# A double-to-single rounding of weight tiles: three VectorE operations in place of five, in a retention and two-layer FFN kernel

## The chip, the cores and the metric

One Trainium2 chip, one core of it. The metric is the device time of one execution of the whole program in microseconds (us). The kernel before took 897.66 us, the median of three runs (896.89 to 899.72).

Engines are named as the profile names them: PE is TensorE (PEld its weight loads), DVE VectorE, ACT ScalarE, POOL GpSimd, SP the engine that issues the DMAs.

## The reference

```python
scores = scale * np.matmul(q, k.transpose(0, 1, 3, 2))          # 4 x 8 heads, 576 positions, 64 wide
ret = scores * Dmat[None, :, :, :]                              # causal decay gamma ** (i - j)
x = np.matmul(ret, v)                                           # -> 2304 tokens x 512
h = x @ w_in;  g = P(h) / (Q(h) + 1e-06);  x = g @ w_out        # layer 1, P cubic, Q quadratic in |h|
h = x @ w_in2; r = np.maximum(h, 0.0)
out = (s * (r * r) + b) @ w_out2                                # layer 2
```

Both layers are 512 to 2048 to 512 wide. The weights arrive as float64, the output is float32.

## The kernel before, in words

**Retention.** Sixteen pairs of heads (`retention`), each with scores, a decay mask, a chunked state and the product with v. DVE makes `pm` (L211), `spre` (L223) and `x` (L242) of each pair; ACT rounds `x` to `xh` (L244) and POOL writes the rest `xl` (L245) and scales `vn` (L190). Nearly all of it stands in program order (`tc.keep_in_program_order`). The loads of pair p+4 are issued at pair p.

**The two layers.** `ffn` walks over units: a block of 256 or 512 tokens by one of 16 slices of 128 hidden columns in each layer, 80 units a layer. `emit_in` (L322 to L324) makes `h` in PSUM with 12 matmuls, from high and low parts of both operands; `rational_*` turn it into `g` in layer 1 (ACT, DVE and POOL), `relu2` in layer 2; `emit_out` (L407) multiplies by the slice's second matrix into `o`, and `evac` adds that to `acc` (L417 or L419). There are `H_BUFS = 4` tiles `h` in PSUM, and in layer 1 the reciprocal is written back into `h` (L356), so unit u+4 can begin on PE only when the last DVE operation of unit u (L363) has read it. Four more PSUM tiles hold `o`.

**The weights.** Tile kf (32 of them, 128 x 1024 doubles, 1 MB) holds both matrices of a slice. `w_load` brings it into one of three `raw` buffers; `w_cut` rounds it. A double is seen as two 32-bit words, `lo` and `hi`, each with a stride of two words. Before, the cut is: ACT takes the absolute value of `hi` read as a float into `wm` (L114), DVE rounds `lo` (L115), clamps `wm` (L117), shifts it (L119), puts the sign in (L121) and ors in the top bits of `lo` (L124, into `hi`). Then ACT copies the result to the fp32r tile `wh` (L130), POOL writes the rest `wl` (L131), and the next load goes out on SP. There is one `wm` buffer (`WTMP_BUFS = 1`), and a slot of `wh` and `wl` comes free when the last unit of tile kf-5 has been multiplied.

**The order.** `w_cut` is a generator that yields after each DVE step. In retention, `steps` chains the cuts of tiles 0 to 2, and each pair from 3 on takes one step (two from 14 on); between the last step of a tile and the first of the next there is no yield. In `ffn`, `emit_cuts` spreads `CUT_STEPS` steps of a tile evenly over the units up to its first use. These calls set only the order of writing there: a scheduler, which is given the program with modelled costs, then sets each engine's queue, and the engines run their queues in order.

Of the kernel before, what the change touches and what calls it, by code (L numbers as in the profile page):

```python
# [11 lines left out]
I32 = mybir.dt.int32  # L12
U32 = mybir.dt.uint32
I64 = mybir.dt.int64
AF = mybir.ActivationFunctionType
ALU = mybir.AluOpType
# [17 lines left out]
G_BUFS = 3  # L34
T_BUFS = {"ta": 2, "tq": 2, "tt": 4}
H_BUFS = 4
CUT_STEPS = 5
W_FIRST = 3
LAG_NS = (5000.0, 4000.0)

# [2 lines left out]
def retention_ffn_kernel(ctx, tc, a, b, s2, b2, w, qkv, maskv, gdec, out):  # L43
    nc = tc.nc
# [31 lines left out]
    def f32(t):  # L76
        return t.bitcast(F32)
# [10 lines left out]
    def next_load(eng=nc.sync, pin=free):  # L88
        if w_ahead:
            w_load(w_ahead.pop(0), eng, pin)  # L90
# [11 lines left out]
    def w_cut(kf, pinned=False):  # L102

        words = w_raw.pop(kf).bitcast(I32).rearrange("p (n two) -> p n two", two=2)
        lo, hi = words[:, :, 0].bitcast(U32), words[:, :, 1]
        f = hi.bitcast(F32)
        m = wtmp.tile([P, 2 * DM], F32, tag="wm", name=f"wm{kf}")
        t = m.bitcast(I32)  # L110

        rest = tc.keep_in_program_order if pinned else free
        pin = tc.keep_in_program_order if kf < W_FIRST + RAW_BUFS else free
        pin(nc.scalar.activation(m, f, AF.Abs))  # L114
        pin(nc.vector.tensor_scalar(lo, lo, 2.0 ** 28, 2.0 ** 32 - 256, op0=ALU.add, op1=ALU.min))  # L115
        yield
        pin(nc.vector.tensor_scalar(m, m, 2.0 ** -15, None, op0=ALU.max))  # L117
        yield
        rest(nc.vector.tensor_scalar(t, t, 5, 2, op0=ALU.logical_shift_left, op1=ALU.logical_shift_right))  # L119
        yield  # L120
        rest(nc.vector.scalar_tensor_tensor(out=t, in0=hi, scalar=-0x40000000, in1=t,  # L121
                                            op0=ALU.bitwise_and, op1=ALU.bitwise_or))
        yield
        rest(nc.vector.scalar_tensor_tensor(out=hi.bitcast(U32), in0=lo, scalar=29, in1=t.bitcast(U32),  # L124
                                            op0=ALU.logical_shift_right, op1=ALU.bitwise_or))
        wh, wl = w_slots[kf % W_BUFS]
        whf, wlf = (x.rearrange("p w c f -> p (w c f)") for x in (wh, wl))
        for which in range(2):
            w_t[kf, which] = (wh[:, which], wl[:, which])
        rest(nc.scalar.copy(whf, f))  # L130
        nc.gpsimd.tensor_tensor(out=wlf, in0=f, in1=f32(whf), op=ALU.subtract)  # L131
        next_load()
# [8 lines left out]
    def retention(actx):  # L141
# [113 lines left out]
        for p in range(1, IN_BUFS):  # L255
            loads(p)
            if p == 2:
                next_load(nc.sync, pin)

        steps = (s for kf in range(W_FIRST) for s in w_cut(kf, True))  # L260


# [29 lines left out]
    def ffn(fctx):  # L292
# [166 lines left out]
        def emit_cuts(u):  # L459

            while items and items[0][1] <= u:
                need, free, kf = items.pop(0)
                assert free < need
                cuts.append([need, CUT_STEPS, w_cut(kf)])
            todo, n = 0, 0
            for need, left, _ in cuts:
                todo += left
                n = max(n, -(-todo // max(need - 1 - u, 1)))
            for _ in range(n):
                cuts[0][1] -= 1  # L470
                next(cuts[0][2], None)
                if not cuts[0][1]:
                    cuts.pop(0)
# [107 lines left out]
```

## Time and profile before

| | |
|---|---|
| three runs | 896.89, 897.66, 899.72 us |
| span of the profiled execution, first to last instruction | 893.9 us |
| busy: PE, PEld | 865.7 (97%), 729.2 us |
| busy: DVE, ACT, POOL | 610.2, 529.4, 360.9 us |
| mean granted clock of PE | 0.997 |

The profile gives the profiled execution by its span; no device time of its own stands beside it. The median lies 3.8 us above that span, which is taken as what lies around it. Times in the views are counted from the span's start. Retention lasts until about 82 us, layer 1 until about 520, layer 2 until the end.

### The profile page before, as it was taken

The numbers are of one execution on the slowest core, as the hardware profiler recorded it, in microseconds if no ns is written. First come the engines' busy times: TensorE is split into PE (matmuls) and PEld (weight loads), VectorE is DVE, ScalarE is ACT, GpSimd is POOL, SyncE is SP. The second block draws the span as 40 slices with busy tenths as digits, with TensorE's granted clock in tenths as the row PEclk, the third lists the DMA queues.
The fourth block names the chain that finished last, engine by engine and source line by source line (L and its number), as shares of the span: only waits on it lengthen the run. The fifth ranks groups of instructions, "written<-read, shape, count | busy, mean of one in ns | idle before, by whom it ended". The sixth has DMA issues, their size and how long they took to land.

```text
span 893.9 us, 12550 instructions
## 1 busy us (share of the span) xinstructions
PE 865.7 (97%) x4896; PEld 729.2 (82%) x4896; DVE 610.2 (68%) x905; ACT 529.4 (59%) x876; POOL 360.9 (40%) x248
## 2 busy tenths in 40 slices
PE   6999999899999999999999899999999999999998
PEld 6988788678788878878888688888888888888886
DVE  4897997999988898888989861545544464333334
ACT  1234997877877877688887664544444444343332
POOL 3776764557565655565788800011111111100000
PEclk9999999999999999999999999999999999999999
DMA  9992110111111101111111110111111110000013
GB/s 339 376 350 96 48 48 1 48 47 48 48 47 48 48 0 48 48 48 48 48 48 48 48 48 0 48 48 48 48 48 47 48 35 14 1 0 1 8 64 141
DMA packets 15418, 58.52 MB, mean 65 GB/s; under 512 B 2176, under 2 KB 2688, under 8 KB 11264
## 3 DMA queue, kind: packets, MB, share of 16 engines
q1 hardware_dynamic: 15360, 57.74, 17.8%
q8 instruction: 38, 0.62, 0.3%
q14 instruction: 20, 0.16, 0.1%
HBM read 53.01 MB, written 4.72 MB: 65 GB/s over the span
## 4 chain that ended last, share of the span: by engine, by line
PE 56%; DVE 17%; ACT 3%; DMA 3%; POOL 2%; issue 1%; DVEq 0%; ACTq 0%
PE o L407 29%; PE h L322 9%; PE h L324 9%; PE h L323 9%; DMA raw<-in_w_dram 3%; DVE acc L419 2%; DVE wm L121 2%; POOL wl L131 2%; DVE raw L124 2%; DVE tt L361 1%; DVE tt L350 1%; DVE h L362 1%; DVE tt L363 1%; DVE wm L119 1%; DVE tt L351 1%; DVE wm L117 1%
## 5 line engine op out<-in xcount | busy, mean ns | idle before, releaser
L322 PE MATMUL h<-xl,wh 128*128 128x512 f32 (+1 forms) x640 | 236.9, 370 | 6.2 <-DVE tt L363 6.1
L324 PE MATMUL h<-xh,wh 128*128 128x512 f32 (+1 forms) x640 | 236.2, 369 | 0.0
L323 PE MATMUL h<-xh,wl 128*128 128x512 f32 (+1 forms) x640 | 236.2, 369 | 0.0
L131 POOL TENSOR_TENSOR wl<-raw,wh 128x1024 fp32r<-128x1024 f32 x32 | 80.4, 2512 | 282.1 <-ACT wh L130 258.2
L380 DVE TENSOR_SCALAR tt<-ta,s_sb,b_sb 128x512 f32<-128x512 f32 (+1 forms) x80 | 47.0, 587 | 153.4 <-ACT ta L379 153.3
L322 PEld LDWEIGHTS h<-xl,wh 128*128 128x128 f32 x640 | 121.0, 189 | 29.2 <-DVE tt L363 4.4
L344 POOL TENSOR_TENSOR tq<-tq,ta 128x512 f32<-128x512 f32 (+1 forms) x80 | 102.1, 1277 | 97.0 <-ACT tq L343 95.1
L323 PEld LDWEIGHTS h<-xh,wl 128*128 128x128 f32 x640 | 121.0, 189 | 20.6
L324 PEld LDWEIGHTS h<-xh,wh 128*128 128x128 f32 x640 | 120.9, 189 | 20.6
L407 PE MATMUL o<-gl,wh 128*128 128x512 f32 (+1 forms) x320 | 118.4, 371 | 4.7 <-POOL gl L373 3.2
L373 POOL TENSOR_TENSOR gl<-tt,gh 128x512 fp32r<-128x512 f32 (+1 forms) x80 | 108.5, 1357 | 35.6 <-ACT gh L368 30.6
L378 ACT ACTIVATE ta<-h 128x512 f32<-128x512 f32 (+1 forms) x80 | 44.5, 557 | 127.7 <-PE h L324 127.6
L407 PE MATMUL o<-gh,wl 128*128 128x512 f32 (+1 forms) x320 | 117.7, 368 | 0.0
L407 PE MATMUL o<-gh,wh 128*128 128x512 f32 (+1 forms) x320 | 116.6, 368 | 0.0
L407 PE MATMUL o<-wh,gl 128*128 128x512 f32 x288 | 112.3, 390 | 0.4 <-DVE gl L383 0.4
L407 PE MATMUL o<-wh,gh 128*128 128x512 f32 x288 | 112.1, 389 | 0.0
L407 PE MATMUL o<-wl,gh 128*128 128x512 f32 x288 | 94.0, 390 | 1.7 <-DVE acc L419 1.7
L383 DVE TENSOR_TENSOR gl<-tt,gh 128x512 fp32r<-128x512 f32 (+1 forms) x80 | 53.2, 665 | 41.1 <-ACT gh L382 41.1
L382 ACT CAST gh<-tt 128x512 fp32r<-128x512 f32 (+1 forms) x80 | 46.3, 579 | 54.3 <-DVE tt L380 52.3
L407 PEld LDWEIGHTS o<-gl,wh 128*128 128x128 f32 x320 | 60.2, 188 | 17.7 <-POOL gl L373 4.7
L419 DVE TENSOR_TENSOR acc<-acc,o 128x512 f32<-128x512 f32 (+1 forms) x114 | 69.6, 650 | 3.3 <-PE o L407 3.3
L361 DVE SCALAR_TENSOR_TENSOR tt<-tt,aneg,h 128x512 f32<-128x512 f32 (+1 forms) x80 | 54.9, 687 | 20.6 <-ACT h L356 20.6
(51 smaller groups left out, 1414.9 us busy)
## 6 DMA issues: line engine op xcount, KB each, us to landing
raw<-in_w_dram SPq DMA_DIRECT2D x32, 1024.0 KB, 4.8
xT<-in_qkv_dram SPq DMA_DIRECT2D x16, 576.0 KB, 8.2
vn<-in_qkv_dram SPq DMA_DIRECT2D x16, 320.0 KB, 8.2
out_dram<-acc SPq DMA_DIRECT2D x18, 256.0 KB, 2.1
kn<-in_qkv_dram SPq DMA_DIRECT2D x16, 256.0 KB, 7.6
mv<-in_maskv_dram SPq DMA_DIRECT2D x1, 310.0 KB, 4.2
odec<-in_gdec_dram SPq DMA_DIRECT2D x1, 256.0 KB, 5.8
a_sb<-in_moe_a_dram SPq DMA_DIRECT2D x1, 2.0 KB, 9.5
```

The lines of the kernel that those rows point to most:

```text
L131: nc.gpsimd.tensor_tensor(out=wlf, in0=f, in1=f32(whf), op=ALU.subtract)
L322: nc.tensor.matmul(ps, lhsT=wh[:, c, :], rhs=xl[:, c, r], start=c == 0, stop=False)
L323: nc.tensor.matmul(ps, lhsT=wl[:, c, :], rhs=xh[:, c, r], start=False, stop=False)
L324: nc.tensor.matmul(ps, lhsT=wh[:, c, :], rhs=xh[:, c, r], start=False, stop=c == NC - 1)
L344: nc.gpsimd.tensor_tensor(out=tq, in0=tq, in1=ta, op=ALU.mult)
L361: nc.vector.scalar_tensor_tensor(out=tt, in0=tt, scalar=aneg[:, 0:1], in1=r, op0=ALU.add, op1=ALU.mult)
L373: nc.gpsimd.tensor_tensor(out=gl, in0=tt, in1=f32(gh), op=ALU.subtract)
L380: nc.vector.tensor_scalar(tt, ta, s2_sb, b2_sb, op0=ALU.mult, op1=ALU.add)
L382: nc.scalar.copy(gh, tt)
L383: nc.vector.tensor_tensor(out=gl, in0=tt, in1=f32(gh), op=ALU.subtract)
L407: nc.tensor.matmul(ps, lhsT=lh, rhs=rh, start=st and x == 0, stop=sp and x == 2)
L419: nc.vector.tensor_tensor(out=at, in0=at, in1=ps, op=ALU.add)
```

## The change

`w_cut` is written with three DVE steps. ACT multiplies `hi`, read as a float, by 2^-112 (`Copy` with a scale, where `Abs` stood); DVE turns `lo` into its top three bits by a multiplication and a minimum (L115), shifts `wm` left by three and ors those bits in (new L117, one operation with two tensor inputs), and puts the sign of `hi` in (new L120, also two inputs). L117 and L119 of before, both with one tensor input, have no counterpart. `CUT_STEPS` goes from 5 to 3, which changes where the steps are written between the units. Lines after the cut are lower by 4 in the new file.

```diff
-CUT_STEPS = 5
+CUT_STEPS = 3
...
-        t = m.bitcast(I32)
+        t = m.bitcast(U32)
...
-        pin(nc.scalar.activation(m, f, AF.Abs))
-        pin(nc.vector.tensor_scalar(lo, lo, 2.0 ** 28, 2.0 ** 32 - 256, op0=ALU.add, op1=ALU.min))
+        pin(nc.scalar.activation(m, f, AF.Copy, scale=2.0 ** -112))
+        pin(nc.vector.tensor_scalar(lo, lo, 2.0 ** -29, 7.0, op0=ALU.mult, op1=ALU.min))
         yield
-        pin(nc.vector.tensor_scalar(m, m, 2.0 ** -15, None, op0=ALU.max))
+        rest(nc.vector.scalar_tensor_tensor(out=t, in0=m.bitcast(U32), scalar=3, in1=lo,
+                                            op0=ALU.logical_shift_left, op1=ALU.bitwise_or))
         yield
-        rest(nc.vector.tensor_scalar(t, t, 5, 2, op0=ALU.logical_shift_left, op1=ALU.logical_shift_right))
-        yield
-        rest(nc.vector.scalar_tensor_tensor(out=t, in0=hi, scalar=-0x40000000, in1=t,
+        rest(nc.vector.scalar_tensor_tensor(out=hi.bitcast(U32), in0=hi.bitcast(U32), scalar=0x80000000, in1=t,
                                             op0=ALU.bitwise_and, op1=ALU.bitwise_or))
-        yield
-        rest(nc.vector.scalar_tensor_tensor(out=hi.bitcast(U32), in0=lo, scalar=29, in1=t.bitcast(U32),
-                                            op0=ALU.logical_shift_right, op1=ALU.bitwise_or))
```

The queues of all engines are laid out anew. PE has the same 4896 matmuls; their interleaving of `h` and `o` differs in layer 1. In retention the cuts of tiles 0 to 2 now end at pair 9, not 14, and on SP `raw2` stands right behind `raw1`, ahead of the inputs of pair 8 (before, behind those of pair 11), `raw4` ahead of those of pair 12 and `raw5` ahead of those of pair 14 (both before behind those of pair 15).

The first place is ACT at the head of layer 1, from the operation on tile 3 on (`ta0`, `tq0` belong to unit 0, `ta1`, `tt1` to unit 1). Before:

```order
L114 ACTIVATE wm3_1083<-raw3_602 128x1024
L342 ACTIVATE ta0_1099<-h0_1086 128x512
L345 ACTIVATE tt0_1101<-h0_1086,aneg_72 128x512
L343 ACTIVATE tq0_1100<-ta0_1099,babs_73 128x512
L342 ACTIVATE ta1_1131<-h1_1118 128x512
L345 ACTIVATE tt1_1133<-h1_1118,aneg_72 128x512
```

Now:

```order
L114 ACTIVATE wm3_1077<-raw3_585 128x1024
L338 ACTIVATE ta0_1093<-h0_1080 128x512
L341 ACTIVATE tt0_1095<-h0_1080,aneg_72 128x512
L339 ACTIVATE tq0_1094<-ta0_1093,babs_73 128x512
L126 CAST wh3_86<-raw3_585 128x1024
L338 ACTIVATE ta1_1125<-h1_1112 128x512
```

The copy `wh3` moved from behind unit 3's exponential to a place ahead of unit 1's first operation; on DVE all three steps of tile 3 now stand ahead of unit 0's first operation, where one of five stood, and the first step of tile 6 stands ahead of unit 1's last operation.

The second place is DVE in layer 1 at unit 15, which with tiles 6 and 7 shares the queue there; its last operation (L363, now L359) lets unit 19 begin on PE. Before:

```order
L351 SCALAR_TENSOR_TENSOR tt15_1781<-tt15_1781,aneg_72,h15_1766 128x512
L117 TENSOR_SCALAR wm6_1941<-wm6_1941 128x1024
L119 TENSOR_SCALAR wm6_1941<-wm6_1941 128x1024
L121 SCALAR_TENSOR_TENSOR wm6_1941<-raw6_1236,wm6_1941 128x1024
L350 TENSOR_TENSOR tt16_1825<-tt16_1825,h16_1810 128x512
L124 SCALAR_TENSOR_TENSOR raw6_1236<-raw6_1236,wm6_1941 128x1024
L361 SCALAR_TENSOR_TENSOR tt15_1781<-tt15_1781,aneg_72,h15_1766 128x512
L362 SCALAR_TENSOR_TENSOR h15_1766<-tq15_1780,h15_1766 128x512
L351 SCALAR_TENSOR_TENSOR tt16_1825<-tt16_1825,aneg_72,h16_1810 128x512
L350 TENSOR_TENSOR tt17_1873<-tt17_1873,h17_1858 128x512
L115 TENSOR_SCALAR raw8_1892<-raw8_1892 128x1024
L363 SCALAR_TENSOR_TENSOR tt15_1781<-h15_1766,tt15_1781 128x512
```

Now:

```order
L347 SCALAR_TENSOR_TENSOR tt15_1771<-tt15_1771,aneg_72,h15_1756 128x512
L117 SCALAR_TENSOR_TENSOR wm6_1929<-wm6_1929,raw6_1146 128x1024
L346 TENSOR_TENSOR tt16_1819<-tt16_1819,h16_1804 128x512
L120 SCALAR_TENSOR_TENSOR raw6_1146<-raw6_1146,wm6_1929 128x1024
L347 SCALAR_TENSOR_TENSOR tt16_1819<-tt16_1819,aneg_72,h16_1804 128x512
L357 SCALAR_TENSOR_TENSOR tt15_1771<-tt15_1771,aneg_72,h15_1756 128x512
L358 SCALAR_TENSOR_TENSOR h15_1756<-tq15_1770,h15_1756 128x512
L117 SCALAR_TENSOR_TENSOR wm7_2161<-wm7_2161,raw7_1284 128x1024
L359 SCALAR_TENSOR_TENSOR tt15_1771<-h15_1756,tt15_1771 128x512
L115 TENSOR_SCALAR raw8_1790<-raw8_1790 128x1024
L120 SCALAR_TENSOR_TENSOR raw7_1284<-raw7_1284,wm7_2161 128x1024
```

Between the two operations on unit 15 stand four operations on weights before (one of them on tile 8) and three now; both steps of tile 7 moved forward, around unit 15's last operation.

The third place is DVE where layer 1 ends: `o77` are the PSUM tiles that PE needs again there, `wm21` is tile 21. Before:

```order
L115 TENSOR_SCALAR raw21_4983<-raw21_4983 128x1024
L363 SCALAR_TENSOR_TENSOR tt79_4807<-h79_4792,tt79_4807 128x256
L117 TENSOR_SCALAR wm21_5393<-wm21_5393 128x1024
L380 TENSOR_SCALAR tt81_4929<-ta81_4928,s2_sb_74,b2_sb_75 128x256
L119 TENSOR_SCALAR wm21_5393<-wm21_5393 128x1024
L121 SCALAR_TENSOR_TENSOR wm21_5393<-raw21_4983,wm21_5393 128x1024
L419 TENSOR_TENSOR acc_1082<-acc_1082,o77_0_4824 128x512
```

Now:

```order
L115 TENSOR_SCALAR raw21_4791<-raw21_4791 128x1024
L117 SCALAR_TENSOR_TENSOR wm21_5317<-wm21_5317,raw21_4791 128x1024
L376 TENSOR_SCALAR tt82_4943<-ta82_4942,s2_sb_74,b2_sb_75 128x256
L415 TENSOR_TENSOR acc_1076<-acc_1076,o77_0_4793 128x512
```

Ahead of the first add of `o77` stand two operations on tile 21 where four stood.

## Rows read from the trace of the kernel before

**Rows 1.** Busy time by stage: length, then busy us (instructions) per engine, PE clock, DMA.
```profile
22.35:82.00 59.65, 56.37 (x963) 51.83 (x960) 50.97 (x70) 18.57 (x32) 44.45 (x28) 1.00 0.76 290
...
156.45:178.80 22.35, 18.39 (x80) 14.94 (x79) 21.54 (x25) 19.37 (x33) 12.26 (x8) 0.92 0.13 48
...
82.00:520.00 438.00, 425.01 (x2037) 354.72 (x2037) 389.83 (x573) 351.69 (x582) 282.66 (x201) 1.00 0.13 46
...
520.00:871.65 351.65, 351.65 (x1631) 294.36 (x1630) 149.21 (x231) 150.19 (x248) 26.71 (x11) 1.00 0.08 29
```

**Rows 2.** Who waited for whom, whole span: total us, times, longest us.
```profile
DVE raw L115 <- DMA raw<-in_w_dram: 22.6, 17, 3.1
...
PE h L322 <- DVE tt L363: 6.1, 4, 4.0
...
PE o L407 <- POOL gl L373: 3.2, 4, 1.2
PE o L407 <- DVE acc L419: 3.2, 3, 1.7
```

**Rows 3.** Groups by line, whole span: busy us, mean ns, then idle before.
```profile
L124 DVE SCALAR_TENSOR_TENSOR raw<-raw,wm 128x1024 uint32<-128x1024 uint32 x32 | 46.0, 1437 | 0.1
L121 DVE SCALAR_TENSOR_TENSOR wm<-raw,wm 128x1024 int32<-128x1024 int32 x32 | 45.2, 1412 | 0.4
...
L119 DVE TENSOR_SCALAR wm<-wm 128x1024 int32<-128x1024 int32 x32 | 30.9, 966 | 0.4
L117 DVE TENSOR_SCALAR wm<-wm 128x1024 f32<-128x1024 f32 x32 | 28.5, 891 | 5.7 <-ACT wm L114 5.6
L115 DVE TENSOR_SCALAR raw<-raw 128x1024 uint32<-128x1024 uint32 x32 | 28.4, 887 | 22.7 <-DMA raw<-in_w_dram 22.6
```

**Rows 4.** Timeline of PE in retention: start us, length us, what.
```profile
28.23 1.33 PE L208 MATMUL sc<-xT 64*128 64x128 f32 x20
...
36.20 1.33 PE L208 MATMUL sc<-xT 64*128 64x128 f32 x20
```

**Rows 5.** Timeline of DVE in retention: the x of five pairs.
```profile
28.63 0.75 DVE L242 TENSOR_TENSOR x<-pv,odec 128x576 f32<-128x576 f32 x1
...
37.25 0.75 DVE L242 TENSOR_TENSOR x<-pv,odec 128x576 f32<-128x576 f32 x1
...
41.72 0.74 DVE L242 TENSOR_TENSOR x<-pv,odec 128x576 f32<-128x576 f32 x1
...
47.15 0.74 DVE L242 TENSOR_TENSOR x<-pv,odec 128x576 f32<-128x576 f32 x1
...
81.99 0.76 DVE L242 TENSOR_TENSOR x<-pv,odec 128x576 f32<-128x576 f32 x1 [1.36 <-PE pv L239]
```

**Rows 6.** Timeline at the head of layer 1, three engines.
```profile
83.61 2.01 DVE L115 TENSOR_SCALAR raw<-raw 128x1024 uint32<-128x1024 uint32 x1
...
86.25 0.81 ACT L343 ACTIVATE tq<-ta,babs 128x512 f32<-128x512 f32 x1
...
92.31 0.69 DVE L363 SCALAR_TENSOR_TENSOR tt<-h,tt 128x512 f32<-128x512 f32 x1
...
97.26 0.50 PE L407 MATMUL o<-gl,wh 128*128 128x512 f32 x1 [1.19 <-POOL gl L373]
```

**Rows 7.** The loads of weight tiles until 120 us.
```profile
DMA to landing us min/median/max: 4.7/5.3/9.5
```

**Rows 8.** Timeline around unit 15, POOL, DVE and PE.
```profile
156.18 2.45 POOL L131 TENSOR_TENSOR wl<-raw,wh 128x1024 fp32r<-128x1024 f32 x1
...
157.19 1.99 DVE L117 TENSOR_SCALAR wm<-wm 128x1024 f32<-128x1024 f32 x1 [0.88 <-ACT wm L114]
...
167.72 0.47 PE L322 MATMUL h<-xl,wh 128*128 128x512 f32 x1 [3.96 <-DVE tt L363]
```

**Rows 9.** Timeline of DVE where layer 1 ends.
```profile
492.58 1.45 DVE L117 TENSOR_SCALAR wm<-wm 128x1024 f32<-128x1024 f32 x1
...
495.26 1.78 DVE L119 TENSOR_SCALAR wm<-wm 128x1024 int32<-128x1024 int32 x1
```

## The prediction

> **What bounds the kernel now.** I read the busy time by stage first, then who waited for whom, then the timelines at the places where PE waits.
>
> The stages [rows 1]: in layer 2 (520 to 871.65) PE is busy for all 351.65 us, so no cheaper cut can shorten it, though 9 of the 32 tiles are cut there. In retention from 22.35 to 82 PE is busy 56.37 of 59.65 us and DVE 50.97. In the stretch with layer 1 (82 to 520) PE is busy 425.0 of 438.0 us and DVE 389.8, or 89%. So PE is the bound, and what the change can give back is PE's idle time where DVE is dense: 13.0 us there, some us in retention, and a stretch at the lower clock: from 156.45 to 178.8 the mean granted clock is 0.92. Between the two levels of 2.4 and 1.2 GHz that is 22.35 x 0.08 x 2 = 3.6 us at the lower one, behind PE's only idle time of about 4 us in the layers, and 1.8 us of work lost.
>
> The waits [rows 2] say who ended PE's idle time: DVE's last operation of a unit (6.1 us in 4 waits, one of 4.0), POOL's `gl` (3.2 in 4), DVE's adds to `acc` (3.2 in 3). Together 12.5 of the 13.0 us.
>
> **The change part by part.**
>
> *What DVE loses.* The two operations that go cost 28.5 and 30.9 us in 32 tiles [rows 3], together 59.4 of DVE's 610.2 us. The three that stay are forms that the trace knows: L115 by its mean of 0.89 us, the two with two inputs by 1.41 and 1.44. A cut falls from 5.6 to 3.7 us. The new arithmetic of L115 and the scaled copy on ACT are in no row. For L115 the bounds are the 0.89 us of today (same form, type and stride) and 1.44 (the rate of two inputs); I take 0.89, since only the arithmetic differs; the upper bound would give 17.6 of the 59.4 us back. ACT's copy I take at the old cost, nothing, with POOL's port and table loads unchanged: the program has one table load, as before. Most of the 59.4 us lies beside PE work and buys nothing: 9 cuts lie in layer 2. It counts at the following places.
>
> *Retention: -1.5 us.* PE needs (36.20 - 28.23) / 2 = 3.99 us a pair where nothing holds it [rows 4]. From the `x` at 28.63 to that at 81.99 there are 12 periods in 53.4 us [rows 5]; at PE's pace 47.8. The 5.5 us over are periods with a long DVE step: 4.47 us for one with a single two-input step (37.25 to 41.72), 5.43 for one with two steps (41.72 to 47.15). Now four periods have one two-input step (+0.4 each) and two have two steps (+1.2, a little under the 1.44 of before), the other six none: 1.6 + 2.4 = 4.0 over, so 1.5 less. Against it, `raw2`, `raw4` and `raw5` go out ahead of inputs that followed or preceded them otherwise. DMA is 0.76 busy there already [rows 1]; the inputs of pairs 14 and 15 come up to two tiles later and POOL's scaling of pair 15 gets close to its need. Bounds: +2.0 (DMA sets the pace) and -4.0 (only the two double steps remain, and their second one is short).
>
> *Head of layer 1: +0.8 us.* ACT's copy `wh3` now stands behind `tq0` (86.25 to 87.06 [rows 6]) and waits for all three steps of tile 3 on DVE. The first of these ran from 83.61 to 85.6; two more at 1.2 end about 88.0, the copy about 89.2, so unit 1's operations on ACT start 1.5 us later than before, and unit 0's last on DVE ends about 95.4, not 93.0 (92.31 + 0.69). Unit 4 on PE starts behind that, now at 95.4 and not at 93.0. But behind unit 4 PE idled 1.19 us for `gl0` and went on at 97.26; `gl0` is now ready at 98.0, and PE comes at 98.1. So 0.8 is what stays. Next in line is the first step of tile 6, whose load `wl3` releases at about 91.7; with the shortest landing of 4.7 us [rows 7] it is there at 96.4, and DVE comes to it at 97.5. Bounds: 0 and +2.6.
>
> *Unit 15: -4.2 us.* This is the long wait. Unit 19 could start on PE at 163.8 and waits until 167.72 for unit 15's last operation [rows 8]. Before it stand the operations of tile 6. The first, at 157.19, took 1.99 us where its kind takes 0.69 alone: POOL's `wl` ran until 158.63. I let the new two-input step end at 158.63 + 1.2 = 159.8, and add the rest of the queue by the pitch of its neighbours: 0.6 + 1.15 + 0.7 + 0.65 + 0.65 + 1.15 (tile 7) + 0.6 = 165.3. PE's wait falls from 4.0 to 1.6 us. The mean clock from 82 to 520 rounds to 1.00, so it falls nowhere else for long, and the other waits in the layers' rows are 1.7 us and less [rows 1, 2]; so the 1.8 us at the lower clock go too: 2.4 + 1.8. Bounds: 0 and -5.8.
>
> The Trainium skill, page "SBUF — State Buffer", section "SBUF: two separate sides", has it that VectorE and GpSimd share a pair of ports under an exclusive lock, held for a whole instruction, which an operation with two SBUF inputs also takes. By that, the new step waits for all of `wl` and this term stands; were only single-input operations held, the step would end at 158.4 and the forecast be 1.4 us lower. The trace agrees as far as it goes: the operation at 157.19 ended 0.55 us behind POOL's.
>
> *The three short waits on a unit's last operation: -1.4 us.* They sum to 6.1 - 4.0 = 2.1 us [rows 2], 0.7 each, less than the 1.9 us by which a cut gets shorter; I count two of three as gone. Bounds: 0 and -2.1.
>
> *End of layer 1: -2.0 us.* PE waits there for PSUM tiles that DVE's adds have yet to empty, 3.2 us in three waits [rows 2]. Ahead of the first add stood the two operations at 492.58 and 495.26, 1.45 + 1.78 = 3.2 us [rows 9]. They go; the first two waits (1.1 and 0.4) with them, of the third, behind the slower `gl` of layer 2, about a third. Bounds: 0 and -3.2.
>
> *What is late next: +1.7 us.* The queues are laid out anew by a scheduler, so waits that do not exist now will appear. Ten waits besides the long one sum to 8.5 us [rows 2], 0.85 each; I add two. The waits on `gl` behind POOL I leave as they are. DVE's 22.6 us of waiting for loads at L115 cost PE nothing today, and the shorter cut does not bring the loads sooner than a free slot allows.
>
> Sum: -1.5 + 0.8 - 4.2 - 1.4 - 2.0 + 1.7 = -6.6 us. The durations come from the profiled execution with its span of 893.9 us, whose own device time is not given; the median of the runs is 897.66, 3.8 above the span. 897.66 - 6.6 = **891.1 us**.
>
> **The rivals.**
>
> *Nothing to measure, 895.7 us.* Three tiles are now cut around units 15 to 18, both steps of tile 7 and those of tile 8 included: DVE reaches unit 16's last operation at about 171.2 where PE would like it at 170.8. If that wait becomes 2.4 us, the retention term is eaten by the loads and the short waits come back in the same number, what is left is 0.8 - 4.2 + 2.4 - 1.0 = -2.0. For it: 17 waits on loads show that the scheduler's picture of the loads is off. Against: DVE's share in layer 1 falls from 89% to about 80% (20 cuts by 1.86 us are 37 us of 438).
>
> *Slower, 901.3 us: first steps held by their loads.* DVE's queue is in order, and the first step of a later tile now stands ahead of operations that PE needs (tile 6 at the head, tile 8 behind unit 15). It decides whether the loads land in 4.7 or 9.5 us, the ends in [rows 7]. With 9.5 tile 6 is there at 101.2, unit 1's last operation ends at 102.6 and PE, which wants it at 100.8, loses 1.8 more. Tile 8, issued at about 158.7, is there at 168.2 where DVE comes at 165.3: 2.9 us more, a wait of 3.3 us on unit 16 and again 1.8 at the lower clock. Then 0.8 + 1.8 - 4.2 + 5.1 = +3.5, with no gain elsewhere: 901.2 to 901.3. Against: outside retention DMA is busy 0.13 [rows 1], and the slow landings belong to its crowded part.
>
> *All DVE waits go, 883.4 us.* Retention -4.0, head +0.8, unit 15 -5.8, short waits -2.1, end of layer 1 -3.2: -14.3.
>
> *The saving is smaller than written:* L115 at 1.44 us. It takes 30% of the DVE time back and with it about 2 us: 893.
>
> **How the numbers follow.** Forecast, the smaller saving included, 0.50; all waits gone 0.12; nothing to measure 0.27; slower 0.11. A measurement of this kernel tells about 0.3%, 2.7 us, from no change. The forecast's own bounds are wide, 886 to 895. The first two cases are faster, the third is same, the fourth slower; a tenth of the forecast falls into same and a tenth of that rival into faster. Faster 0.62, same 0.27, slower 0.11. The range from 883 to 899 takes in the third case and nearly all of the second, and leaves out the fourth and a part of the second.
>
> **What would show it.** In the profile after: DVE about 550 us busy; groups of the cut of 32 at 0.9, 1.4 and 1.4 us; PE busy the same but for the lower clock; no clock below 1.00 between 82 and 520; waits of `h` on DVE's last operation under 3 us in all; the last `x` about 1.5 us earlier. Wrong would be: a PE wait of 3 us or more on a unit behind a held first step, or a retention that ends no sooner with DMA busy to its end.

## The result, and the profile after

The changed kernel took **884.71 us**, the median of four runs (884.0 to 885.55), against 897.5 us for the kernel before in the same session: a ratio of 0.9852, 95% interval 0.9837 to 0.9868, or 12.8 us less. The forecast was 891.1, so the direction was right and the change twice as large as forecast; the time lies near the lower end of the range, 1.3 us above what the rival "all DVE waits go" gave.

The span of the profiled execution fell from 893.9 to 883.8 us. DVE is busy 560.3 us (610.2 before), PE 862.8, ACT 529.2, POOL 351.9.

Busy time by stage, kernel after (columns as in [rows 1]): retention, the stretch with layer 1, layer 2.

```profile
22.35:82.72 60.37, 56.95 (x966) 53.02 (x962) 45.21 (x63) 18.81 (x32) 46.73 (x29) 0.97 0.79 305
82.72:509.90 427.18, 421.97 (x2037) 355.18 (x2038) 357.84 (x533) 351.11 (x582) 271.35 (x199) 1.00 0.13 45
509.90:861.50 351.60, 351.60 (x1631) 294.33 (x1630) 137.27 (x212) 150.34 (x248) 26.73 (x11) 1.00 0.08 29
```

The second row holds the same 2037 PE instructions as the third of [rows 1], which took 438.0 us from the last `x` at 81.99. So the stretch with layer 1 gave 10.8 us, retention took 0.7 more, and layer 2 took what it took before. Of the 10.8 us, 7.8 are idle time of PE (13.0 before, 427.18 - 421.97 = 5.2 now), and 3.0 are busy time: 425.0 us for 2037 instructions before, 422.0 now.

Who waited for whom, kernel after (total us, times, longest us), beside [rows 2]:

```profile
DVE raw L115 <- DMA raw<-in_w_dram: 21.6, 21, 2.9
...
PE h L318 <- DVE tt L359: 4.5, 4, 1.9
...
PE pv L215 <- issue: 2.4, 2, 1.7
...
PE o L403 <- DVE gl L379: 0.6, 1, 0.6
```

PE waits for POOL's `gl` and for DVE's `acc` no more; of the waits on a unit's last operation four are left, none of them longer than 1.9 us. They and the one on `gl` of layer 2 are all that the timeline of PE has behind 90 us, together 5.1 us:

```profile
94.96 0.50 PE L318 MATMUL h<-xl,wh 128*128 128x512 f32 x1 [1.25 <-DVE tt L359]
...
166.66 0.47 PE L318 MATMUL h<-xl,wh 128*128 128x512 f32 x1 [1.93 <-DVE tt L359]
...
391.85 0.39 PE L318 MATMUL h<-xl,wh 128*128 128x256 f32 x1 [0.38 <-DVE tt L359]
394.49 0.38 PE L318 MATMUL h<-xl,wh 128*128 128x256 f32 x1 [0.95 <-DVE tt L359]
508.52 0.50 PE L403 MATMUL o<-wh,gl 128*128 128x512 f32 x1 [0.62 <-DVE gl L379]
```

The start of the first matmul of a unit in the two timelines of PE says where the time came from (worked out from both). When these seven units start, PE has run the same number of matmuls in both kernels. For others that does not hold, since the two interleave `h` and `o` differently (before unit 80, 12 fewer in the kernel after, which is 2.7 us):

```
unit            0       16      24      36      70      89     159
before       81.81   152.54  196.62  262.93  427.99  531.66  878.53
after        82.54   153.51  195.64  259.65  422.33  521.57  868.41
difference   +0.73    +0.97   -0.98   -3.27   -5.65  -10.09  -10.12
```

The cut's groups by line, kernel after (columns as in [rows 3]), and POOL's `gl`:

```profile
L117 DVE SCALAR_TENSOR_TENSOR wm<-wm,raw 128x1024 uint32<-128x1024 uint32 x32 | 47.5, 1484 | 8.4 <-ACT wm L114 8.2
...
L120 DVE SCALAR_TENSOR_TENSOR raw<-raw,wm 128x1024 uint32<-128x1024 uint32 x32 | 43.0, 1343 | 0.3
L115 DVE TENSOR_SCALAR raw<-raw 128x1024 uint32<-128x1024 uint32 x32 | 30.1, 940 | 21.6 <-DMA raw<-in_w_dram 21.6
...
L369 POOL TENSOR_TENSOR gl<-tt,gh 128x512 fp32r<-128x512 f32 (+1 forms) x80 | 100.3, 1257 | 36.6 <-ACT gh L364 25.6 <-issue 10.0 <-POOL tq L340 0.7
```

The same POOL group in the kernel before, 100 ns longer each time:

```profile
L373 POOL TENSOR_TENSOR gl<-tt,gh 128x512 fp32r<-128x512 f32 (+1 forms) x80 | 108.5, 1357 | 35.6 <-ACT gh L368 30.6 <-DVE h L362 2.5 <-issue 1.5
```

The five groups of before sum to 179.0 us, the three of now to 120.6, a difference of 58.4 (59.4 forecast). DVE's busy time fell by only 49.9. The engine total counts time, the groups count each operation from start to end, and on DVE these overlap: in the timeline at unit 15 below, the operation at 160.54 lasts 0.68 us and the next starts 0.60 after it. Added up over all operations of DVE (worked out from the traces) this overlap was 48.9 us and is 42.2, which is 6.7 of the 8.5 us between the two figures; the other operations took 1.8 us longer.

### The profile page after: what moved, and what is told of

The parts are those of the page before. It is cut to its first block, busy times and chain, and to the rows that moved or that the text cites. A ratio compares the mean times of both kernels' runs of the same rounds, so it can differ in the third digit from the quotient of the medians.

```text
span 883.8 us, 12510 instructions
## 1 busy us (share of the span) xinstructions
PE 862.8 (98%) x4896; PEld 730.4 (83%) x4896; DVE 560.3 (63%) x841; ACT 529.2 (60%) x876; POOL 351.9 (40%) x248
## 4 chain that ended last, share of the span: by engine, by line
PE 81%; DVE 7%; ACT 4%; DMA 4%; issue 2%; POOL 2%; SPq 0%; DVEq 0%; POOLq 0%; ACTq 0%
PE o L403 39%; PE h L318 13%; PE h L319 13%; PE h L320 13%; DMA vn<-in_qkv_dram 2%; DMA raw<-in_w_dram 2%; DVE acc L415 1%; DVE wm L117 1%; PE pv L235 1%; PE sc L204 1%; DVE raw L120 1%; PE pv L215 1%; PE pv L227 1%; POOL tq L340 1%; ACT h L352 1%
## 5 line engine op out<-in xcount | busy, mean ns | idle before, releaser
L340 POOL TENSOR_TENSOR tq<-tq,ta 128x512 f32<-128x512 f32 (+1 forms) x80 | 100.2, 1253 | 101.4 <-ACT tq L339 101.3
L369 POOL TENSOR_TENSOR gl<-tt,gh 128x512 fp32r<-128x512 f32 (+1 forms) x80 | 100.3, 1257 | 36.6 <-ACT gh L364 25.6
```

What stands on the lines that cost most here:

```text
L340: nc.gpsimd.tensor_tensor(out=tq, in0=tq, in1=ta, op=ALU.mult)
L369: nc.gpsimd.tensor_tensor(out=gl, in0=tt, in1=f32(gh), op=ALU.subtract)
```

## The experiments

"Operations that change no value" are a maximum with -4 and a shift by 0, both on `wm`: they take VectorE's time and leave the result as it is.

**Two operations back.** The three-operation cut with the work of five.

```diff
-CUT_STEPS = 3
+CUT_STEPS = 5
...
+        pin(nc.vector.tensor_scalar(m, m, -4.0, None, op0=ALU.max))
+        yield
+        rest(nc.vector.tensor_scalar(m.bitcast(I32), m.bitcast(I32), 0, 0, op0=ALU.logical_shift_left, op1=ALU.logical_shift_right))
+        yield
```

> The changed kernel with two single-input VectorE operations per tile put back that change no value (a maximum with -4, a shift by 0), at the places and with the yields of before, CUT_STEPS 5: the queues of PE are those of before. Theory 1 (the time that VectorE no longer spends is what counts): back to 897 us, within 2. Rival (the scaled copy on ScalarE or the new arithmetic of L115 pays): stays at or below 893.

Measured 896.39 us, before 897.18: ratio 0.9990 (0.9977 to 1.0003). The waits of PE in the layers are those of before, one by one:

```profile
PE h L322 <- DVE tt L363: 6.3, 5, 4.0
...
PE o L407 <- POOL gl L373: 3.4, 4, 1.2
PE o L407 <- DVE acc L419: 3.1, 3, 1.7
```

So the scaled copy on ACT and the new arithmetic are worth nothing that these runs can tell from zero (0.8 us); the gain is VectorE's two operations and the steps that go with them, which this run takes back together. The four waits on POOL's `gl`, too, are here and not in the kernel after.

**One operation back.** The maximum alone, `CUT_STEPS` 4.

> As before it, with one of the two no-value operations (the maximum), CUT_STEPS 4. Theory 1: about half of the gain is left, 890 to 893 us, and PE's waits on VectorE's last operation of a unit lie between those of the two kernels. Rival (the new layout of the queues happened to be good): no order by dose, the time may lie outside 885 to 897.

Measured 893.91 us (890.95 to 895.53), ratio 0.9956 (0.9939 to 0.9974). The first operation that goes buys 896.4 - 893.9 = 2.5 us, the second 9.2. The expected half of the gain (890 to 893) did not come, nor waits between those of the two kernels: PE waits 10.0 us on a unit's last operation, more than before (6.1) and after (4.5). One of the five waits is at unit 19 as before, the others are at units 46, 54, 70 and 80. So the gain is not so many us for each operation; where the waits fall depends on the queues too, and `CUT_STEPS` 4 lays these out anew. Of the waits on `gl` one is left, with POOL's `gl` as long as before:

```profile
PE h L320 <- DVE tt L361: 10.0, 5, 3.2
...
PE o L405 <- POOL gl L371: 1.7, 1, 1.7
...
L371 POOL TENSOR_TENSOR gl<-tt,gh 128x512 fp32r<-128x512 f32 (+1 forms) x80 | 109.1, 1367 | 33.8 <-ACT gh L366 21.0
```

**The change, written in the old places.** `CUT_STEPS` 5 with the three-operation cut, which alters only where the steps are written between the units; the queues differ in many places.

> The changed kernel with CUT_STEPS 5 and no other edit: the three steps are written between the units as if there were five, so earlier. Theory 1: 885 us within 2, since the work is the same. Rival (layout): 889 or more.

Measured 884.73 us (884.27 to 885.39), ratio 0.9852 (0.9832 to 0.9872), the time of the change. PE's waits stand elsewhere (0.94 at 297.5, 0.96 at 497.0) and sum to the same. So with three operations the changed `CUT_STEPS` has no part in the gain.

**Five operations in three steps.** The old cut, with its second to fourth operation written as one step, `CUT_STEPS` 3.

```diff
         pin(nc.vector.tensor_scalar(m, m, 2.0 ** -15, None, op0=ALU.max))
-        yield
         rest(nc.vector.tensor_scalar(t, t, 5, 2, op0=ALU.logical_shift_left, op1=ALU.logical_shift_right))
-        yield
         rest(nc.vector.scalar_tensor_tensor(out=t, in0=hi, scalar=-0x40000000, in1=t,
```

> The kernel before with its five operations written in three steps (L117, L119 and L121 together) and CUT_STEPS 3. Theory 1: 897 us within 2, or worse by some us, since three operations in a row hold VectorE for 3 us. Rival (layout): much of the gain appears without removing an operation, 891 or less.

Measured 903.45 us, before 897.18: ratio 1.0061 (1.0043 to 1.0078), 6.3 us slower by the medians. In its timeline PE idles three times in retention, as a step of three operations ran ahead of an `x`:

```profile
37.38 1.34 PE L217 MATMUL pv<-vn,kn 128*64 128x128 f32 x16 [2.90 <-issue]
50.83 1.14 PE L217 MATMUL pv<-vn,kn 128*64 128x128 f32 x16 [3.70 <-issue]
64.26 0.95 PE L217 MATMUL pv<-vn,kn 128*64 128x128 f32 x16 [3.59 <-issue]
```

The last `x` comes at 92.06 (81.99 before). Retention cares how much DVE work stands ahead of one `x`, not how much there is in all.

The layers tell something else. From unit 24 to unit 70, with as many matmuls of PE as in the kernel before, this kernel took 5.1 us less (worked out from the starts, 210.00 to 436.28), though no VectorE operation is gone. The three short waits on a unit's last operation that stood there are gone, and of the four waits on `gl` one is left:

```profile
PE o L405 <- POOL gl L371: 1.2, 1, 1.2
...
L371 POOL TENSOR_TENSOR gl<-tt,gh 128x512 fp32r<-128x512 f32 (+1 forms) x80 | 106.5, 1331 | 28.1 <-ACT gh L366 20.9
```

So in that stretch another order of the steps does what the change does. It does not do it elsewhere: the wait ahead of unit 19 is 5.18 us, and the waits on `acc` at the end of layer 1 are those of before (1.09, 0.41 and 1.66).

**No pair with two steps.** The change, with a yield more between the tiles that are cut in retention, so that no pair of heads takes the last step of one tile and the first of the next.

```diff
         next_load()
+        if pinned:
+            yield
```

> The changed kernel with one more yield at the end of a cut in retention, so that no pair has two VectorE steps (its nine steps lie in pairs 3 to 11); the loads of tiles 4 and 5 come a few pairs later by that. Theory 1 (retention gained nothing because two pairs have two steps in a row, of which one is followed by a stretch at the lower clock): the last x of retention comes at 80 us or before, not 82.7, and the time is 881 to 883. Rival (the earlier loads of weights set retention's pace): no change, 884 to 885.5.

Measured **882.52 us** (882.37 to 882.72), ratio 0.9839 (0.9815 to 0.9863): faster than before, and 2.2 us under the change, none of whose runs came below 883.78. Retention, from 22 us to its last `x` at 79.76:

```profile
22.00:79.77 57.77, 55.80 (x965) 51.72 (x960) 45.02 (x64) 18.57 (x32) 47.47 (x30) 1.00 0.84 318
```

PE's clock stays at 1.00 (0.97 in the first row of after), the idle of 1.67 us is gone, and the layers are those of the change, 3 us earlier.

**Low words left out.** No L115; L117 shifts without the bits of `lo`, so it has one tensor input, and the weights lose their last bits.

> The changed kernel without L115, and with a single-input shift in place of the operation that ors the low words in: the low words are not used, so the weights lose their last bits. VectorE has two operations a tile. The loads stand as in the changed kernel. Theory 1 (PE's waits follow VectorE's time): PE's waits of 5 us between 80 and 508 fall under 2, retention ends by 80, and the time is 876 to 881. Rival (what is left are waits of another kind, on ScalarE, GpSimd or the loads): 883 or more.

Measured 880.71 us (880.28 to 881.48), ratio 0.9819 (0.9798 to 0.9840). The operation that is gone and the one that is cheaper buy 4.0 us more (884.71 - 880.71). The time came as expected, two signs did not: the last `x` is at 81.12 and not by 80, and PE's waits are 3.5 us and not under 2. Behind 80 us two are left, 0.73 at 92.8 and the one ahead of unit 19, which is longer than the 1.93 of the change, with less work on VectorE:

```profile
164.82 0.67 PE L316 MATMUL h<-xl,wh 128*128 128x512 f32 x1 [2.76 <-DVE tt L357]
```

**Old work in retention alone.** The two operations that change no value in tiles 0 to 2 only; then the reverse, in tiles 3 to 31 only, with `if not pinned` and `CUT_STEPS` 5; the change itself and the first run again beside the second. The first edit:

```diff
+        if pinned:
+            pin(nc.vector.tensor_scalar(m, m, -4.0, None, op0=ALU.max))
+            yield
+            rest(nc.vector.tensor_scalar(m.bitcast(I32), m.bitcast(I32), 0, 0, op0=ALU.logical_shift_left, op1=ALU.logical_shift_right))
+            yield
```

> The changed kernel with the two no-value operations and the yields of before in tiles 0 to 2 alone, those that are cut in retention. Theory 1: retention ends as in the kernel before, at 82.0, so the time is 883.5 to 885 and all of the gain lies in the layers. Rival (a part of the gain comes from retention in runs without a profile): 887 or more.

Measured 887.25 us (885.49 to 888.2), ratio 0.9889 (0.9865 to 0.9912): the rival's time.

> The reverse of the run before: tiles 0 to 2, which are cut in retention, have the new cut of three operations, and tiles 3 to 31 the new cut with two VectorE operations added that change no value, so that the layers have VectorE's old amount of work. Theory A (what the profiled executions show: retention ends 0.7 us later with the new cut, everything is gained in the layers): within 1 us of the kernel with the two operations in all tiles, so 0.8 us below the kernel before, ratio 0.998 to 1.000. Theory B (in most executions the old retention takes some 2 us more than in the profiled one, so the new cut gains 2 to 2.5 us there): 2.8 to 3.3 us below the kernel before, ratio about 0.9965. In the trace of both: the waits of the layers as before (about 4 us in front of unit 19), last x at 82 to 83 us.

Measured 895.06 us (893.97 to 896.68), before 896.73: ratio 0.9979 (0.9970 to 0.9989), between the two theories. Its waits in the layers are those of before, but for two short ones on a unit's last operation:

```profile
PE h L323 <- DVE tt L364: 4.6, 2, 4.0
PE o L408 <- POOL gl L374: 3.2, 4, 1.2
PE o L408 <- DVE acc L420: 3.2, 3, 1.6
```

> The changed kernel itself, for a comparison on one chip with the two runs beside it. Theory A: equal to the kernel with the old amount of work in retention alone (within 0.7 us), and 12 us below the kernel with the old amount in the layers alone. Theory B: 2 to 2.5 us below the former, and 9.5 to 10 us below the latter. Time 884.7 us, ratio 0.985 by both.

Measured 885.15 us, ratio 0.9863 (0.9848 to 0.9879).

> The kernel with the old amount of VectorE work in tiles 0 to 2 alone, on the same chip as the change and with more rounds, since its profiled execution was the lowest of four and the changed kernel's the highest of four. Theory A: 884.7 us, like the change. Theory B: 886.7 to 887.3 us, 2 to 2.5 above it.

Measured 888.35 us (886.54 to 889.22), ratio 0.9898 (0.9883 to 0.9914).

So the cheaper cut in the layers alone is worth 8.4 us (888.35 against 896.73; 9.6 in the first measurement), in retention alone 1.7, and the two together 11.6 to 12.8. With the layers cut anew, the new cut of tiles 0 to 2 is worth 3.2 us by the medians (888.35 - 885.15). Yet no profile shows retention end sooner by it: the last `x` comes at 82.29 to 82.72 in the four kernels with that cut (the change twice, written early, retention alone) and at 81.99 to 82.52 in the four with the old amount of work (before, two back, old retention twice). What the profiles do show is at the head of layer 1: with the old work in retention PE waits 1.81 and 2.14 us ahead of unit 4 (1.25 and 1.20 in the change), behind 2.14 at a granted clock of 0.64 from 95.2 to 100, and up to unit 16 that is 0.6 and 2.0 us more than in the change. The profiled executions were the lowest of their runs for the kernel with the old retention both times (886.54, 885.49) and the highest for the change (885.44, 885.55); what differs in the other executions stays open.

## Why the prediction came out half as large

The direction was right, and PE's waits on DVE were the right place. The size was not: the forecast time was 6.4 us too long. Of these, 3.5 us lie in the sum (-6.6 forecast, -10.1 between the two profiled executions), above all in the waits on `gl`, put at nothing, and in pricing waits by recorded idle time; the other 2.8 or so lie in where the two profiled executions stand among their runs. Two terms that missed the other way, by 2.2 us each in retention and at unit 15, hide a part of it: from unit 24 to 89 the sum had -1.7, and -9.1 were measured.

**The time of the profiled execution.** The step "the median lies 3.8 us above that span, which is taken as what lies around it" was wrong. In each run whose span is listed the time is 1.7 to 2.2 us above the span (885.55 and 883.8, 896.55 and 894.8), so the profiled execution of before took about 895.7 us and was a quick one. The sum was made on an execution that lacked some 2 us of what the median had to lose; that of after, 885.55, lies 0.84 above its median.

**What DVE loses**: 58.4 us in the groups, as forecast but for 1.0; L115 took 0.94, near the chosen 0.89 and not 1.44. "DVE about 550 us" was wrong by 10, since it took a sum of groups off an engine total, and DVE's share in the stretch with layer 1 fell to 84% (357.84 of 427.18), not to about 80%.

**The sum, place by place**, measured by the starts of the units above:

| term | forecast | measured |
|---|---|---|
| retention | -1.5 | +0.7 |
| head of layer 1 (to unit 16) | +0.8 | +0.2 |
| unit 15 (unit 16 to 24) | -4.2 | -2.0 |
| short waits, POOL's `gl` (unit 24 to 70) | -1.4 and 0 | -4.7 |
| end of layer 1 (unit 70 to 89) | -2.0 | -4.4 |
| what is late next | +1.7 | in the rows above |
| sum | -6.6 | -10.1 |

Of the signs named in the prediction the groups of the cut came true. DVE's total, PE's busy time (2.9 us less), the clock between 82 and 520, the 3 us of waits of `h` (4.5) and the last `x` did not. (Its own tenths would have made the chances of faster and same 0.60 and 0.29, not 0.62 and 0.27.)

*Retention.* The price of a pair with two steps, "+1.2, a little under the 1.44 of before", failed. Timeline of the kernel after, DVE, POOL and PE:

```profile
42.54 0.75 DVE L238 TENSOR_TENSOR x<-pv,odec 128x576 f32<-128x576 f32 x1
...
46.01 1.64 DVE L120 SCALAR_TENSOR_TENSOR raw<-raw,wm 128x1024 uint32<-128x1024 uint32 x1
...
46.53 2.39 POOL L241 TENSOR_TENSOR xl<-x,xh 128x576 fp32r<-128x576 f32 x1
47.57 1.90 DVE L115 TENSOR_SCALAR raw<-raw 128x1024 uint32<-128x1024 uint32 x1
...
49.39 0.74 DVE L238 TENSOR_TENSOR x<-pv,odec 128x576 f32<-128x576 f32 x1
...
50.24 0.89 PE L215 MATMUL pv<-vn,kn 128*64 128x128 f32 x16 [1.67 <-issue]
...
51.52 1.87 PE L235 MATMUL pv<-pm,vn 128*64 128x128 f32 x18 [0.21 <-DVE pm L207]
...
82.72 0.76 DVE L238 TENSOR_TENSOR x<-pv,odec 128x576 f32<-128x576 f32 x1 [1.36 <-PE pv L235]
```

The period is 49.39 - 42.54 = 6.85 us where 5.2 were forecast: POOL's `xl` ran into both steps, and L115, which takes 0.69 us alone (at 83.46), took 1.90. PE then idled 1.67 us, and from 51.4 to 54.9 its granted clock was 0.57. (The other such pair took 5.40 us, from 33.67 to 39.07.) The spread variant, which takes that pair away, shows what the term could have been: its last `x` comes 2.2 us before that of the kernel before. By the medians of the last runs the new cut of tiles 0 to 2 gains 1.7 to 3.2 us, but no profile places that ahead of the last `x`; whether the 1.5 forecast for retention came true in the other executions is not shown.

The Trainium skill, page "SBUF — State Buffer", section "SBUF: two separate sides", says that a GpSimd operation and a VectorE operation that has two SBUF inputs or runs in a two-port mode take the port pair they share as a lock: the one that starts first holds it for its whole instruction, the other is blocked. The trace agrees here: L120, which has two SBUF inputs, started first and ended at 47.65; `xl`, 1.41 us long at 23.86, where no step of a cut ran, started at 46.53 and ended at 48.92, 1.27 behind L120, and L115 ended 0.55 us behind `xl`. Whether L115 runs in a two-port mode no run here shows.

*Unit 15.* The mechanism was right, the clock was not. Timeline of DVE, then POOL, then PE, kernel after:

```profile
157.77 2.85 DVE L117 SCALAR_TENSOR_TENSOR wm<-wm,raw 128x1024 uint32<-128x1024 uint32 x1 [1.15 <-ACT wm L114]
160.54 0.68 DVE L346 TENSOR_TENSOR tt<-tt,h 128x512 f32<-128x512 f32 x1
161.14 1.73 DVE L120 SCALAR_TENSOR_TENSOR raw<-raw,wm 128x1024 uint32<-128x1024 uint32 x1
...
164.70 1.21 DVE L117 SCALAR_TENSOR_TENSOR wm<-wm,raw 128x1024 uint32<-128x1024 uint32 x1
165.84 0.68 DVE L359 SCALAR_TENSOR_TENSOR tt<-h,tt 128x512 f32<-128x512 f32 x1
...
157.07 2.47 POOL L127 TENSOR_TENSOR wl<-raw,wh 128x1024 fp32r<-128x1024 f32 x1
...
168.70 0.63 PE L319 MATMUL h<-xh,wl 128*128 128x512 f32 x1
169.13 0.63 PE L320 MATMUL h<-xh,wh 128*128 128x512 f32 x1
```

The new L117 waited for all of POOL's `wl` and ended 1.08 us behind it, as the sum had it; `wl` ended 0.9 later than in the kernel before. The wait fell from 3.96 to 1.93 us (1.6 forecast). But "so the 1.8 us at the lower clock go too" failed: matmuls start 0.43 us apart from 168.3 to 170.8, where 0.23 is their pitch, and the windows show a granted clock of 0.56 from 167.5 to 171.1. The term was a wait of 2.0 us, without the 1.8.

*The short waits and `gl`.* Here lies the largest part of the miss. "The waits on `gl` behind POOL I leave as they are" was wrong: no wait on it is left, and with VectorE's two operations back all four return. And all three short waits went, not two. POOL's `gl` takes 1257 ns where it took 1357, but its length does not decide: with one operation back it takes 1367 and one wait on it is left, with five operations in three steps 1331 and one. What is left is when its inputs come off VectorE's queue. How much of that is the work that is gone and how much the order of the steps is open, since five operations in three steps took 5.1 us less than before in this stretch, where the change took 4.7 less.

*End of layer 1.* All three waits on `acc` went, and one of 0.19 us on `gl` (at 484.22) with them; the bound was 3.2 us and 4.4 were measured, which brings up the step under all of these.

**A wait of PE is worth more than the idle time that the trace gives it.** All terms in the layers were sums of recorded idle time. Timeline of PE, kernel before, on both sides of the long wait (the matmul between them is in [rows 8]):

```profile
163.14 0.39 PE L323 MATMUL h<-xh,wl 128*128 128x512 f32 x1
163.37 0.39 PE L324 MATMUL h<-xh,wh 128*128 128x512 f32 x1
...
168.03 0.46 PE L323 MATMUL h<-xh,wl 128*128 128x512 f32 x1
```

Matmuls take 0.39 us and start 0.23 apart. From 163.37 to 167.72 are 4.35 us, 4.12 over the pitch, where 3.96 are recorded: the last matmul ran out alone, for 0.16 us that count as busy. The first one behind the wait starts 0.31 before its successor, 0.08 more than the pitch (0.34 and 0.11 behind the wait at 94.96 in the kernel after, whose successor starts at 95.30). That is about 0.26 us a wait. The stretch with layer 1 had 14 waits in the kernel before, the shortest included, and has 6 now: 8 x 0.26 = 2.1 of the 3.0 us by which PE's busy time fell. By the starts in the two timelines some 0.4 us more were single matmuls that came late without any recorded idle time, since a delay under 0.16 us leaves none; the last 0.5 is spread over all of them. Counted from start to start (worked out from the traces, against a pitch of 0.227 us for 512 columns and 0.120 for 256), PE lost 19.5 us from unit 0 to 89 before and 8.7 now, and the difference is the 10.8 us whole: 2.0 and 2.2 up to unit 16, 5.8 and 3.8 up to 24, 6.4 and 1.8 up to 70, 5.3 and 0.9 up to 89.

**What is late next.** "I add two" (+1.7) came near: two new waits exist (0.38 and 0.95 at 391.85 and 394.49, 1.3 us of idle), where two on `gl` stood.

**The rivals.** "First steps held by their loads" did not come: PE waits nowhere in the layers behind a held first step for over 1.9 us. "Nothing to measure" needed a wait of 2.4 us behind unit 16's last operation, and there is none. "All DVE waits go" came nearest; it failed at unit 15 and in retention's double steps.

## What to carry to other kernels

Where the bound engine waits in many small places, count a wait from start to start of its instructions, not by recorded idle, and ask of each waiting engine whether the shortened one stands in its way or feeds it: a third engine's waits can vanish with the work taken off the second. Place the forecast's profiled execution in the spread of the runs first: time minus span is nearly constant over the runs, so a span alone tells which one it was. Compare two kernels by the start of an instruction only where the engine has done the same work in both. And work that runs between two deadlines is priced by the longest piece between them: retention is 2.2 us shorter than before when no piece is doubled, and 10.1 us longer when three are joined.

## What the runs showed of the hardware

The clock of PE fell to the lower level behind some waits of 1.7 to 2.6 us and not behind others of 1.9 to 3.2, and the length of the wait alone does not tell which. In the kernel with the old retention (first measurement) the granted clock was 1.00 from 166.70 to 172.00, behind an idle time of 1.91 us, at the place where the change fell to 0.56 behind 1.93. With one operation back it stayed at 1.00 from 168 to 173, behind 3.19 us, and was 0.66 from 351 to 356, behind 2.59.

What a stretch at the lower clock costs can come back where the engine would have waited soon after. In the kernel with the new cut in retention alone the mean clock from 168 to 180 us was 0.75, 12 x 0.25 = 3.0 us of work lost. PE idled 0.77 us at 201.0 and 0.69 at 231.4 in the kernel before; in this one those waits are gone, and from unit 24 to 36 it took 2.3 us less. That VectorE caught up in the meantime would fit, but no run shows that alone: those waits are gone in the kernel with five operations in three steps too.
